# Attention and mixture of experts on one core: 804 slots for 816, and eight small moves in the schedule

## The chip, the core and the metric

The kernel runs on one core of one Trainium2 chip. The time is the device time of one launch in microseconds (us), and of several launches the median. A launch reads all inputs from the chip's main memory (HBM) and writes the output there. The profile is that of one further execution, recorded by the hardware profiler.

## The reference

Two layers follow one another. The first is attention over 4 batches, 8 heads, 768 positions and 64 elements a head: each query sees the keys within 15 positions of it, and beside them 24 summary keys, one for each block of 32 keys.

```
k_sum = k.reshape(B, H, nb, block, D).max(axis=3)
v_sum = v.reshape(B, H, nb, block, D).mean(axis=3)
scores_l = scale * q @ k^T          # kept where |i - j| < 16, else -1e9
scores_s = scale * q @ k_sum^T + log(32)
a = softmax(concat(scores_l, scores_s))
x = a @ concat(v, v_sum)
```

The result is read as 3072 tokens of 512 elements. The second layer sends each token to two of eight experts, chosen by noisy logits, and adds up what the two return.

```
noisy = x @ w_gate + log1p(exp(x @ w_noise)) * noise
two largest of each row -> experts, softmax over the two -> weights
out[token] += weight * (relu(x[token] @ w1[e]) @ w2[e])     # 512 -> 1024 -> 512
```

With 6144 places for eight experts an expert gets 768 tokens on average.

## The kernel before

**Attention** is worked through in 24 tiles of 128 queries, six to a batch. One turn of the loop, step t, holds work of several tiles: the division of tile t-1 (norm, L368), the scores and row maxima of tile t+2 (L322, L334), the transposes of the probabilities of tile t+1 (p_trans, L346), the exponentials of t+2 (sexp, L338), and the products with V of tile t in two halves (av, L357). Beside these stand side works. They are given to a list with a step number and a fraction, `at(t, f, ...)`, and the loop calls `run` with fixed fractions in a fixed order: 0.02, 0.03, 0.5, 0.1, 0.2, 0.09, 0.3, 0.32, 0.6, 0.85, 0, 0.8, 0.9. So a work at 10.85 stands near the end of step 10, ahead of one at 10.9, and one at 11 near the end of step 11. The works that the change touches:

- `load_k` (L107) brings the keys of a batch, two of its four head pairs at a time; `KL` says in which steps. The keys are kept in two buffers, one batch each. `k_piece` (L226) takes their block maxima on DVE; `KP` says when (the last batch in steps 11 to 14, third and fourth piece at 13.1 and 14.1).
- `kx_local` and `kx_sum` (L118, L126) copy the keys that one tile needs, and the block maxima, into one of `QN` buffers. The maxima are only copied for the first `QN` tiles of a batch, since they stay in the buffer.
- `v_sums` (L255) forms the block means of V on PE and copies them to the last 24 rows of a V buffer; `v_rest` (L287) copies them from there with DMAs to the other V windows (five for the third and the fourth batch). For the third batch the first stands at 10.6 and the second at 11.02. The products with V of a tile read both windows of its buffer.
- `w_load` (L664) brings a quarter of w1 or w2 of an expert (512 KB) into one of four stage buffers; `W0` says when the four w1 loads of expert 0 come. `w_part` (L686) then makes of each half a float16 high part on ACT and a float16 rest, the low half, on DVE.
- `norm_hi`, `norm_hi_dve`, `norm_lo` (L380 to L391) write a finished tile as a high and a low float16 part to one of three `xr` buffers, on ACT or DVE and on POOL; `x_out` (L393) stores it to HBM.
- `gate_f` and `gate_t` (L583, L590) build and multiply one-hot tables that tell for each slot of an expert which token it holds; `gate_t` is eight matmuls on PE, in the spare columns of the bank that holds a tile's result.

Each engine works its instructions off in the order of the program. All loads and stores of the attention stage are issued by SP's queue, in program order as well. At the start 90 products of the identity with itself (`warm_up`, L245) keep PE at work until the keys are there.

**Experts.** Each expert has `CAP` slots. The tokens of its slots are gathered with indirect DMAs in chunks of 128 (`x_gather`, seven chunks, `NCH`), and transposed with a DMA (`x_trans`, L813), the last chunk only as far as `CAP` reaches. The first layer of experts 1 to 7 (`mm1_all`, L887) is a seven-product scheme for a 2 x 2 split of its matrices (Strassen's): the slots are split in halves of `HC = CAP // 2`, and `product` (L858) runs each product as six matmuls of 128 x 128 by 128 x HC: high by high, low by high and high by low, two row groups each. Expert 0 uses the plain form (`mm1_pe`, L830), with the first `H0` = 384 slots ahead of the rest. The second layer takes chunks of 128 slots and 512 output columns (`mm2_pass`, L985); its last chunk has 64 slots, split into two column halves. What does not fit into `CAP` slots would be worked off in a branch at the end (L1452), which is entered only if an expert has more tokens than slots.

Of the kernel before, what the change touches and what calls it, by code (L numbers as in the profile page):

```python
# [9 lines left out]
F16 = mybir.dt.float16  # L10
# [10 lines left out]
P = 128  # L21
# [3 lines left out]
DM = H * D  # L25
E, F = 8, 1024
FC = F // P
DC = DM // P
# [3 lines left out]
PAD = WIN - 1  # L32
KW = 2 * (PAD + 1) + HP * S
VP = S + W - 64
H0, CAP = 384, 816
HF, HC = F // 2, CAP // 2
QN = 3
QBUF = 5
QA = 4
WARM = 90  # L40
SK = HP * NK
SW = 16 * (D + 1)
NCH = 7
# [17 lines left out]
def attn_moe(ctx, tc, qt, kt, vt, wgn, noise, w1, w2, out):  # L61
    nc = tc.nc
# [13 lines left out]
    moe = ctx.enter_context(tc.tile_pool(name="moe", bufs=1))  # L76
# [3 lines left out]
    work = works.enter_context(tc.tile_pool(name="work", bufs=2, side="right"))  # L80
# [19 lines left out]
    for i in range(2):  # L100
        KB.append(keep.tile([P, KW], F32, name=f"kb{i}"))
    for i in range(QN):
        KX.append(keep.tile([P, HP, 2, NK], F32, name=f"kx{i}"))
# [14 lines left out]
    def kx_local(t):  # L118
        b, j = divmod(t, TS)
        for blk in range(2):  # L120
            c = j * P + 64 * blk
            r = max(0, c + W - S)
            k = KB[b % 2][:, r:r + HP * S].rearrange("p (h s) -> p h s", h=HP)
            nc.gpsimd.tensor_copy(KX[t % QN][:, :, blk, 0:W], k[:, :, c - r:c - r + W])

    def kx_sum(t):  # L126
        b, j = divmod(t, TS)
        if j < QN:
            (nc.gpsimd if b else nc.vector).tensor_copy(KX[t % QN][:, :, :, W:NK],
                                                        KM[b][:, :, None, :].to_broadcast([P, HP, 2, NB]))  # L130
# [24 lines left out]
    identb = const.tile([P, P], BF, name="identb")  # L155
# [57 lines left out]
    late = []  # L213
# [29 lines left out]
    VO = []  # L243

    def warm_up(n):  # L245
# [2 lines left out]
            nc.tensor.matmul(o[:, i % 2, 0:P], identb, identb, start=True, stop=True, skip_group_check=True)  # L248
        VO.append(o)

    C4 = 2 * (D + 1)

    PV = {}
# [5 lines left out]
    def v_sums_pe(b):  # L259
# [5 lines left out]
        for j in range(TS):  # L265
            for g in range(4):
                nc.tensor.matmul(pt[32 * g:32 * g + NB, 0:C4], ind[:, j, :], VN[j][:, C4 * g:C4 * g + C4],  # L267
                                 start=(j == 0), stop=(j == TS - 1), skip_group_check=True)
# [35 lines left out]
    SC, PE_, PT, PO, X, XR, XT = {}, {}, {}, {}, {}, {}, {}  # L304
# [18 lines left out]
    def scores(t):  # L323
        s, q, k = SC[t], QR[t], KX[t % QN]
        for hp in range(HP):
# [54 lines left out]
    def norm_hi(t):  # L380
        if t in XR:
            return
        XR[t] = work.tile([P, 2 * DM], F16, name="xr", bufs=3)
        nc.scalar.activation(XR[t][:, 0:DM], X[t], AF.Copy)  # L384

    def norm_hi_dve(t):
        XR[t] = work.tile([P, 2 * DM], F16, name="xr", bufs=3)
        nc.vector.tensor_copy(XR[t][:, 0:DM], X[t])

    def norm_lo(t, engine=nc.gpsimd):  # L390
# [199 lines left out]
    def gate_t(b, o, i=1):  # L590
        tb = o[:, i, GO:GO + 3 * NS]
        n = (BATCH[b][1] - BATCH[b][0]) // GN
        for h in range(n):
            lh, rh, _ = GR[b, h]
            for j in range(GN):
                for k in range(2):
                    nc.tensor.matmul(tb, lh[:, 2 * j + k], rh[:, 2 * j + k],
                                     start=(h + k + j == 0), stop=(h == n - 1 and k == 1 and j == GN - 1),
                                     skip_group_check=True)
# [47 lines left out]
    def w_alloc(e):  # L647
        w1_alloc(e)
        w2_alloc(e)
# [127 lines left out]
    XTE = {}  # L777
# [34 lines left out]

    def x_trans(e, c):  # L813
        if c == 0:
            XTE[e] = (late[0] if e % 2 else moe).tile([P, 2 * DC, CAP], F16, name="xte")
        n = min(P, CAP - c * P)
        nc.sync.dma_start_transpose(out=XTE[e][:, :, c * P:c * P + n], in_=XC[e, c][:n])

    XC = {}
# [228 lines left out]
    def at(t, f, *a):  # L1048
        todo.setdefault(round(t, 3), []).append((f, a))
# [8 lines left out]

    warm_up(WARM)
    for t in range(1, 3):  # L1060
# [10 lines left out]
    at(0.1, v_sums_out, 0)  # L1071

    w_alloc(0)
    W0 = [6, 7, 11, 12]
    SPLIT = [7, 9, 13, 15]
    for i in range(4):
        at(W0[i], w_load, 0, i)
        for k in range(2):
            at(SPLIT[i] + k + 0.9, w_part, i, k, 0)
            at(SPLIT[i] + k + 2.1, w_part, i, k, 1)  # L1080
    VS = [4, 10, 16]
    KP = ((1, 1, 2, 2), (5, 6, 8, 8), (11, 12, 13, 14))
    KL = ((-1, 0), (3, 6), (9, 11))
    VL = [(1, 2), (7, 8), (13, 14)]
    for b in range(B - 1):
        for h in range(HP):
# [12 lines left out]
    for b, (t0, t1) in enumerate(BATCH[:4]):  # L1099
        u = t1 + 2  # L1100
        at(u - 0.15, gate_gt, b)
        at(u + 0.02, gate_gc, b)
        at(u + 0.09, gate_gl, b)
        at(u + 0.09, gate_gd, b)
        at(u + 0.9, gate_a, b)
        at(u + 1.1, gate_b, b)
        at(u + 1.1, gate_m, b)
        at(u + 1.9, gate_p, b)
        at(u + 2.3, lambda b, t: gate_c(b, PO[t]), b, u + 2)
        at(u + 3.02, lambda b, t: gate_d(b, PO[t]), b, u + 2)  # L1110
        at(u + 3.1, gate_e, b)
        if b == 3:
            break
        z = u + (6 if b < 2 else 4)
        at(z + 0.1 if b else u + 4.1, gate_v, b)
        at(z + (0.2 if b < 2 else 1.02), gate_o, b)
        at(z + 1.03, gate_f, b)
        at(z + 1.32, lambda b, t: gate_t(b, PO[t]), b, z + 1)
        at(z + 2.02, lambda b, t: gate_u(b, PO[t]), b, z + 1)
    at(20.1, decode, TB0, 0, 3)  # L1120
    at(20.85, gate_gt, 4)
# [17 lines left out]
    for t in range(-2, NT - 1):  # L1139
        if 3 <= t + QA < NT:  # L1140
            load_q(t + QA)
        if 1 <= t < NT - 2:
            v_load(t + 2)
        u = t + 3
        if t >= 1:
            norm(t - 1, (lambda: kx_sum(u)) if u < NT else None)
        run(t + 0.02)
        run(t + 0.03)
        if t + 2 < NT:
            scores(t + 2)  # L1150
        if 1 < u < NT and t < 1:
            q_piece(u)
        run(t + 0.5)
        if t + 2 < NT:
            smax(t + 2)
        if t in DVE_HI:
            norm_hi_dve(t - 1)
        if 0 <= t + 1 < NT:
            p_trans(t + 1, 0)
            p_trans(t + 1, 1)  # L1160
        if t + 3 < NT:
            mask_sums(t + 3)
        if t + 2 < NT:
            sexp(t + 2, 0)
        if u < NT and t >= 1:
            kx_local(u)
        run(t + 0.1)
        run(t + 0.2)
        if t >= 0:
            av_space(t)  # L1170
            av(t, range(H // 2))
        if t >= 1:
            x_pe(t - 1)
        run(t + 0.09)
        run(t + 0.3)
        run(t + 0.32)
        if t >= 1:
            x_copy(t - 1)
        if t + 2 < NT:
            sexp(t + 2, 1)  # L1180
        if t >= 1:
            norm_hi(t - 1)
            norm_lo(t - 1)
        if t >= 0:
            av(t, range(H // 2, H))
        run(t + 0.6)
        run(t + 0.85)
        run(t)
        run(t + 0.8)
        run(t + 0.9)  # L1190
        if t >= 2:
            x_out(t - 2)
# [142 lines left out]
    for e in range(1, E):  # L1335
# [8 lines left out]
        n = e + 1  # L1344
# [53 lines left out]
    def over_chunk(e, c):  # L1398
        tb = moe.tile([P, 2], I32, name="tbo", bufs=1)
        nc.sync.dma_start(tb, table[bass.ds(c * P + (e * R + CAP), P)])  # L1400
        idx = bass.IndirectOffsetOnAxis(ap=tb[:, 0:1], axis=0)
        x = XG[0]
        indirect(out=x, out_offset=None, in_=xd, in_offset=idx, bounds_check=N - 1, oob_is_err=False)
        pv = PREV[0]
        indirect(out=pv, out_offset=None, in_=out, in_offset=idx, bounds_check=N - 1, oob_is_err=False)
        xt = moe.tile([P, 2 * DC, CAP], F16, name="xte")[:, :, :P]
        nc.sync.dma_start_transpose(out=xt, in_=x)
        hh, hl = [x[:, :, :P] for x in HT]
        w = WT[e]
        for f in range(FC):  # L1410
            ph = bank()[:, 0, :P]
            k = 0
            for wn, xo in (("w1h", 0), ("w1l", 0), ("w1h", DC)):
                for d in range(DC):
                    nc.tensor.matmul(ph, w[wn][:, d, f * P:(f + 1) * P], xt[:, xo + d, :],
                                     start=(k == 0), stop=(k == 11))
                    k += 1
            nc.scalar.activation(hh[:, f, :], ph, AF.Relu)
            nc.vector.scalar_tensor_tensor(hl[:, f, :], ph, 0.0, hh[:, f, :], op0=OP.max, op1=OP.subtract)
        py = psum.tile([P, 512], F32, name="pt", bufs=2)  # L1420
        k = 0
        for wn, hx in (("w2h", hh), ("w2l", hh), ("w2h", hl)):
            for f in range(FC):
                wv = w[wn].rearrange("p a (b d) -> p (a b) d", d=DM)
                nc.tensor.matmul(py, hx[:, f, :], wv[:, f, :], start=(k == 0), stop=(k == 23))
                k += 1
        y = side_pool[0].tile([P, DM], F32, name="y", bufs=3)
        nc.vector.scalar_tensor_tensor(y, py, tb.bitcast(F32)[:, 1:2], pv, op0=OP.mult, op1=OP.add)
        indirect(out=out, out_offset=idx, in_=y, in_offset=None, bounds_check=N - 1, oob_is_err=False)
# [73 lines left out]
```

## Time and profile before

| | us |
|---|---|
| median of 3 runs (lowest, highest) | 659.13 (658.93, 660.64) |
| the profiled execution | 661.28 |
| its span, first to last instruction | 659.5 |
| PE busy in the span | 640.2 |
| DVE, ACT, POOL busy | 486.3, 319.3, 331.2 |
| attention: until the first product of expert 0 | 142.0 |
| expert 0: until the first product of expert 1 | 212.7 |

A row of the timeline has the start and the length in us, the engine, the line, the operation, the tiles (written <- read), the shape and the number of instructions in a run; in square brackets is the time that the engine stood idle before it and what ended that. A row of the chain of waits in order of time has start, length, engine, tile and line. A row of busy time by stretch has the stretch, its length, the busy time and number of instructions of PE, weight loads, DVE, ACT and POOL, then the granted clock of TensorE (1.00 is full), the busy share of the DMA engines and GB/s. A row of a group has the busy time of all its instructions and the mean of one in ns.

### The profile page before, as it was taken

The numbers are of one execution on the slowest core, as the hardware profiler recorded it, in microseconds if no ns is written. First come the engines' busy times: TensorE is split into PE (matmuls) and PEld (weight loads), VectorE is DVE, ScalarE is ACT, GpSimd is POOL, SyncE is SP. The second block draws the span as 40 slices with busy tenths as digits, with TensorE's granted clock in tenths as the row PEclk, the third lists the DMA queues.
The fourth block names the chain that finished last, engine by engine and source line by source line (L and its number), as shares of the span: only waits on it lengthen the run. The fifth ranks groups of instructions, "written<-read, shape, count | busy, mean of one in ns | idle before, by whom it ended". The sixth has DMA issues, their size and how long they took to land.

```text
span 659.5 us, 14051 instructions
## 1 busy us (share of the span) xinstructions
PE 640.2 (97%) x5407; PEld 372.2 (56%) x5407; DVE 486.3 (74%) x867; ACT 319.3 (48%) x677; POOL 331.2 (50%) x473
## 2 busy tenths in 40 slices
PE   7999899989999999999999999999999999999996
PEld 6777677755555554555455445544654555455543
DVE  5768889977788689587958795788678777856511
ACT  3889898753342653255326523542454155415400
POOL 5365444541856548563856376546556551632042
PEclk9999999999999999999999999999999999999999
DMA  8999997999998765536645664557257713431031
GB/s 301 307 298 319 286 326 254 288 257 363 243 191 166 228 190 160 205 116 194 168 162 177 160 198 151 182 157 229 96 190 164 239 70 113 144 126 49 1 106 44
DMA packets 104675, 125.58 MB, mean 190 GB/s; under 512 B 58525, under 2 KB 59813, under 8 KB 104600
## 3 DMA queue, kind: packets, MB, share of 16 engines
q1 hardware_dynamic: 92456, 88.32, 45.7%
q0 software_dynamic: 12144, 36.28, 17.3%
q8 instruction: 44, 0.72, 0.5%
q14 instruction: 31, 0.25, 0.1%
HBM read 87.57 MB, written 26.21 MB: 173 GB/s over the span
## 4 chain that ended last, share of the span: by engine, by line
PE 87%; ACT 4%; DMA 4%; DVE 3%; issue 1%; SPq 1%; POOL 1%; POOLq 0%; DVEq 0%
PE pt L994 37%; PE h L875 26%; PE h L839 5%; PE a L875 4%; PE pt L991 3%; PE s L329 2%; DMA kb<-in_kt_dram 2%; PE o L362 2%; PE pt L349 2%; ACT p L343 2%; PE pt L399 1%; DMA xg<-xd,tb 1%; PE h L994 1%; ACT pts L352 1%; PE pt L267 1%
## 5 line engine op out<-in xcount | busy, mean ns | idle before, releaser
L92 POOL DMA_INDIRECT out_dram<-y,tb x48 | 66.3, 1381 | 152.5 <-DVE y L1017 141.3
L994 PEld LDWEIGHTS <-hth 128*128 128x128 f16 x768 | 74.9, 98 | 89.2
L994 PE MATMUL pt<-w2h,hth 128*128 128x512 f16 x376 | 88.8, 379 | 0.0
L994 PE MATMUL pt<-w2h,htl 128*128 128x512 f16 x376 | 88.8, 379 | 0.0
L994 PE MATMUL pt<-w2l,hth 128*128 128x512 f16 x376 | 88.8, 379 | 0.0
L92 POOL DMA_INDIRECT xg<-xd,tb x53 | 70.4, 1328 | 31.3 <-DVE oc L614 17.4
L875 PE MATMUL h<-tx,sh 128*128 128x408 f16 x336 | 78.6, 336 | 0.0
L1017 DVE SCALAR_TENSOR_TENSOR y<-pt,tb,prev 128x512 f32<-128x512 f32 x42 | 31.5, 749 | 51.9 <-PE pt L994 51.9
L697 DVE SCALAR_TENSOR_TENSOR w2l<-stg,w2h 128x1024 f16<-128x1024 f32 x32 | 49.6, 1558 | 27.3 <-ACT w2h L680 27.3
L994 PEld LDWEIGHTS <-htl 128*128 128x128 f16 x384 | 37.6, 98 | 45.3
L875 PEld LDWEIGHTS <-w1h 128*128 128x128 f16 x448 | 43.3, 98 | 33.8 <-issue 1.4
L744 POOL TENSOR_TENSOR t<-xte 128x816 f32<-128x816 f16 x24 | 41.1, 1739 | 36.9 <-DVE t L700 31.6
L391 POOL TENSOR_TENSOR xr<-x,xr 128x512 f16<-128x512 f32 x24 | 28.9, 1205 | 59.4 <-ACT xr L384 36.7
L92 POOL DMA_INDIRECT prev<-out_dram,tb x42 | 51.9, 1236 | 13.6 <-issue 13.6
L875 PE MATMUL h<-xte,w1h 128*128 128x408 f16 x224 | 57.0, 336 | 0.0
L343 ACT ACTIVATE p<-s,nm 128x120 f32<-128x120 f32 x192 | 53.7, 378 | 0.8
L897 ACT ACTIVATE p<-h 128x408 f32<-128x408 f32 x28 | 14.3, 511 | 73.7 <-PE h L875 72.4
L772 ACT ACTIVATE tx<-t 128x816 f16<-128x816 f32 x28 | 24.0, 879 | 50.8 <-DVE t L700 50.8
L875 PEld LDWEIGHTS <-sh 128*128 128x128 f16 x336 | 32.9, 98 | 25.1
L875 PE MATMUL h<-tx,sl 128*128 128x408 f16 x168 | 42.7, 336 | 0.0
L883 DVE SCALAR_TENSOR_TENSOR htl<-h,hth 128x408 f16<-128x408 f32 x56 | 32.2, 575 | 8.3 <-ACT hth L880 8.2
L725 ACT ACTIVATE sh<-ws 128x1536 f16<-128x1536 f32 x14 | 20.8, 1483 | 35.7 <-DVE ws L700 27.7
(220 smaller groups left out, 1240.0 us busy)
## 6 DMA issues: line engine op xcount, KB each, us to landing
stg<-in_w_dram SPq DMA_DIRECT2D x62, 512.0 KB
q<-in_qt_dram SPq DMA_DIRECT2D x24, 256.0 KB
hth<-in_vt_dram SPq DMA_DIRECT2D x8, 768.0 KB
xd<-xr SPq DMA_DIRECT2D x24, 256.0 KB
out_dram<-prev SPq DMA_DIRECT2D x8, 768.0 KB
kb<-in_kt_dram SPq DMA_DIRECT2D x6, 768.0 KB
vw<-in_vt_dram SPq DMA_DIRECT2D x16, 260.0 KB
vw<-in_vt_dram SPq DMA_DIRECT2D x16, 130.0 KB
```

Source lines behind the costliest of these rows:

```text
L92: return nc.gpsimd.indirect_dma_start(**kw)
L343: nc.scalar.activation(PE_[t][:, a, hp, :], SC[t][:, a, hp, :], AF.Exp, bias=NM[t][:, 1, a, hp:hp + 1], scale=0.125)
L391: engine.tensor_tensor(XR[t][:, DM:], X[t], XR[t][:, 0:DM], op=OP.subtract)
L697: nc.vector.scalar_tensor_tensor(lo, SG[e, i], sc, hi, op0=OP.mult, op1=OP.subtract)
L725: nc.scalar.activation(h, x, AF.Copy, scale=W1S)
L744: nc.gpsimd.tensor_tensor(tt(e, 0 if low else j), xb(e, *i, low), xb(e, *o, low), op=OP.subtract)
L772: nc.scalar.activation(TX[e][:, 0, j - 1], t_of(e, j), AF.Copy)
L839: nc.tensor.matmul(ph[:, :n], w[wn][:, c, f * P:(f + 1) * P], x[:, xo + c, c0:c1], start=(k == 0), stop=(k == 11), skip_group_check=hook i ...
L875: nc.tensor.matmul(o, lhs[a][:, c], rhs[b][:, c], start=start and n == 0, stop=stop and n == 5, skip_group_check=True)
L883: nc.vector.scalar_tensor_tensor(HT[1][:, f, c0:c1], c, 0.0, HT[0][:, f, c0:c1], op0=OP.max, op1=OP.subtract)
L994: nc.tensor.matmul(py, hx[:, f, c * P:c * P + P], w[:, f, :], start=first, stop=final, skip_group_check=True)
L1017: nc.vector.scalar_tensor_tensor(y, py[:, :d], gw, pv[:, :d], op0=OP.mult, op1=OP.add)
```

## The change

`CAP` goes from 816 to 804, and with it `HC` from 408 to 402. The transposed tokens keep their width of 816 (`XCAP`), and the DMA transpose of the last chunk still takes 48 rows, of which 36 are gathered; the rest of the row is not read. `QN` goes from 3 to 2, the `xr` buffers from 3 to 4. There are 100 warming products for 90, and ten more after the scores of tile 1 and ahead of the transposes of tile 0. The third w1 load of expert 0 stands at 10.9 for 11, the second half of the last batch's keys at 10.85 for 11. The low halves of w1 stood at 9.1, 10.1, 11.1, 12.1, 15.1, 16.1, 17.1, 18.1 and now stand at 10.1, 10.2, 13.1, 13.2, 15.1, 16.1, 18.1, 19.1. The table product of the third group of tiles stands at 19.6 for 19.32, behind the second half of the products with V.

```diff
-H0, CAP = 384, 816
+H0, CAP = 384, 804
+XCAP = 816
 HF, HC = F // 2, CAP // 2
-QN = 3
+QN = 2
 QBUF = 5
 QA = 4
-WARM = 90
+WARM = 100
...
+    def keep_warm(n):
+        for i in range(n):
+            nc.tensor.matmul(VO[0][:, 1, 0:P], identb, identb, start=True, stop=True, skip_group_check=True)
+
...
     def norm_hi(t):
         if t in XR:
             return
-        XR[t] = work.tile([P, 2 * DM], F16, name="xr", bufs=3)
+        XR[t] = work.tile([P, 2 * DM], F16, name="xr", bufs=4)
...
     def x_trans(e, c):
         if c == 0:
-            XTE[e] = (late[0] if e % 2 else moe).tile([P, 2 * DC, CAP], F16, name="xte")
-        n = min(P, CAP - c * P)
+            XTE[e] = (late[0] if e % 2 else moe).tile([P, 2 * DC, XCAP], F16, name="xte")
+        n = min(P, XCAP - c * P)
...
-    W0 = [6, 7, 11, 12]
+    W0 = [6, 7, 10.9, 12]
     SPLIT = [7, 9, 13, 15]
+    LOW = ((10.1, 10.2), (13.1, 13.2), (15.1, 16.1), (18.1, 19.1))
     for i in range(4):
         at(W0[i], w_load, 0, i)
         for k in range(2):
             at(SPLIT[i] + k + 0.9, w_part, i, k, 0)
-            at(SPLIT[i] + k + 2.1, w_part, i, k, 1)
+            at(LOW[i][k], w_part, i, k, 1)
     VS = [4, 10, 16]
     KP = ((1, 1, 2, 2), (5, 6, 8, 8), (11, 12, 13, 14))
-    KL = ((-1, 0), (3, 6), (9, 11))
+    KL = ((-1, 0), (3, 6), (9, 10.85))
...
-        at(z + 1.32, lambda b, t: gate_t(b, PO[t]), b, z + 1)
+        at(z + (1.32 if b < 2 else 1.6), lambda b, t: gate_t(b, PO[t]), b, z + 1)
...
         if t in DVE_HI:
             norm_hi_dve(t - 1)
+        if t == -1:
+            keep_warm(10)
         if 0 <= t + 1 < NT:
             p_trans(t + 1, 0)
             p_trans(t + 1, 1)
```

More of the change, by code (lines that the diff above doesn't have):

```diff
@@ L382, in norm_hi @@
             return
-        XR[t] = work.tile([P, 2 * DM], F16, name="xr", bufs=3)
+        XR[t] = work.tile([P, 2 * DM], F16, name="xr", bufs=4)
         nc.scalar.activation(XR[t][:, 0:DM], X[t], AF.Copy)
     def norm_hi_dve(t):
-        XR[t] = work.tile([P, 2 * DM], F16, name="xr", bufs=3)
+        XR[t] = work.tile([P, 2 * DM], F16, name="xr", bufs=4)
         nc.vector.tensor_copy(XR[t][:, 0:DM], X[t])
@@ L1405, in over_chunk @@
         indirect(out=pv, out_offset=None, in_=out, in_offset=idx, bounds_check=N - 1, oob_is_err=False)
-        xt = moe.tile([P, 2 * DC, CAP], F16, name="xte")[:, :, :P]
+        xt = moe.tile([P, 2 * DC, XCAP], F16, name="xte")[:, :, :P]
         nc.sync.dma_start_transpose(out=xt, in_=x)
```

## The prediction

> **What bounds the kernel now.** I read the page's summary and its chain of waits first, then that chain in order of time, and last the timeline and the busy time by stretch of the stages that the edits touch.
>
> ```profile
> span 659.5 us, 14051 instructions
> PE 640.2 (97%) x5407; PEld 372.2 (56%) x5407; DVE 486.3 (74%) x867; ACT 319.3 (48%) x677; POOL 331.2 (50%) x473
> PE 87%; ACT 4%; DMA 4%; DVE 3%; issue 1%; SPq 1%; POOL 1%; POOLq 0%; DVEq 0%
> ```
>
> TensorE sets the end for 87% of the span. How evenly it does so in the experts is seen in the chain in order of time (start, length, what, how many), and in the busy time of the stretch from 212 us on.
>
> ```profile
> 176.85 17.52 PE h L839 x96
> ...
> 227.25 12.42 PE h L875 x72
> 241.74 31.08 PE pt L994 x144
> 212.00:660.00 448.00, 441.06 (x2532) 231.23 (x2528) 316.71 (x430) 182.07 (x296) 223.99 (x293) 1.00 0.50 150
> L875 PE MATMUL h<-tx,sh 128*128 128x408 f16 x336 | 78.6, 336 | 0.0
> ```
>
> From 212 us PE is busy 441 of 448 us, DVE 317, ACT 182, POOL 224, and the products stand end to end: 12.42/72 = 172.5 ns for 408 columns, 17.52/96 = 182.5 ns for 432. So a column costs (182.5 - 172.5)/24 = 0.417 ns. (The 336 ns of one product is its latency; products overlap, and no idle time stands before them.) A column taken out here is time taken off the end. In the attention stage, up to 142 us, the chain changes between PE, ACT, DVE and transfers, so there an edit is worth what its own step says.
>
> **804 slots.** The seven-product scheme of experts 1 to 7 runs 7 experts x 4 row blocks x 7 products x 6 matmuls = 1176 matmuls, each half of the slots wide: 402 columns for 408. That is 6 x 0.417 = 2.5 ns each, 2.94 us in all. Expert 0's second half falls from 432 to 420 columns in 96 matmuls: 96 x 12 x 0.417 = 0.48 us. Sum **-3.42 us**. The second layer does not change: its last chunk is computed 64 slots wide in both kernels. What DVE, ACT and POOL save on 402 columns lies beside PE. The other end of the bound is that the narrower slices stream no faster (0); I take the full 3.42, since the two rows that bracket it, 408 and 432, lie on PE without idle time. In the reference's own draw of inputs the fullest expert gets 801 tokens and expert 0 ends at slot 748, so 804 suffices and the overflow branch, 48 table writes at some 1.4 us each and eight weight reloads, stays shut.
>
> The rows above were taken with slices that begin at multiples of 816 bytes; 804 leaves 4 bytes over a multiple of 16. The Trainium skill, "SBUF — State Buffer", section "Specifications (TRN2)", says that SBUF is read in lines of 16 bytes and that each crossing into a new line pays a penalty; by that rule a shifted slice touches one line more, no run here shows such a slice, and the sum would lose part of the 3.42 us. It is the third rival below.
>
> **Warming products.** Ten more stand at the start and ten between the scores and the first transposes of tile 0.
>
> ```profile
> 1.55 6.92 PE L248 MATMUL o<-identb 128*128 128x128 bf16 x90 [1.55 <-DVE identb L156]
> ...
> 10.73 0.44 PE L329 MATMUL s<-kx,q 64*64 64x120 f32 x8 [1.10 <-DVE kx L241]
> 11.20 1.05 PE L329 MATMUL s<-kx,q 64*64 64x120 f32 x32
> 13.10 2.09 PE L349 MATMUL pt<-ident,p 128*120 128x128 f32 x8 [0.84 <-ACT p L343]
> 15.30 1.68 PE L329 MATMUL s<-kx,q 64*64 64x120 f32 x32
> 16.91 2.64 PE L267 MATMUL o<-hth 128*24 128x130 f32 x48
> 22.39 1.05 PE L329 MATMUL s<-kx,q 64*64 64x120 f32 x32
> 70.53 1.53 PE L267 MATMUL pt<-hth 128*24 128x130 f32 x48 [0.79 <-ACT xt L405]
> 8.60:12.00 3.40, 2.30 (x72) 1.82 (x68) 3.10 (x7) 0.00 (x0) 2.83 (x8) 1.00 1.06 410
> 12.00:15.40 3.40, 2.56 (x27) 1.37 (x23) 1.64 (x3) 2.92 (x11) 0.36 (x1) 1.00 1.08 332
> 15.40:18.90 3.50, 3.50 (x74) 2.87 (x70) 1.16 (x1) 2.64 (x10) 0.00 (x0) 0.51 0.98 232
> ```
>
> Ten products at 6.92/90 = 77 ns are 0.8 us. The first ten lie under the 1.10 us that the scores wait for the keys at 10.73, the other ten in the 0.84 us before 13.10, where PE waits for ACT: cost **0**, and 1.6 us if both covers went. What they could gain: from 15.4 to 18.9 the granted clock is 0.51. The scores there take 1.68 us instead of 1.05, the V sums 2.64 instead of 1.53: 1.7 us at most. The stretch before it (12.0 to 15.4) had PE busy 2.56 of 3.40 us and lost the clock all the same; the one before, with 2.30, kept it. So busy time as such doesn't decide, and whether 0.8 us more would is not shown. I take **0** (the row as it stands) and keep -1.7 for the range.
>
> The Trainium skill, "TensorE: Matmul & The Clock Gate", Part 4, says that transposes do not count as busy for the clock, which fits the eight transposes that fill most of the stretch lost. Part 1 adds that the windows run free of the kernel's start, which speaks against a steady gain: the same ten products would fall on another side of a window from run to run. By the rule that activity holds the clock the sum would be 1.7 us lower, by the free-running window it would be so in some executions only.
>
> **The two loads one step sooner.** The second half of the last batch's keys and the third w1 load go from after step 11's copies of the V sums (L292) to before step 10's x_out, on SP's queue.
>
> ```profile
> 69.12 0.61 SPq L301 DMA_DIRECT2D vw<-in_vt_dram  x1
> 70.41 0.33 SPq L394 DMA_DIRECT2D xd<-xr  x1
> ...
> 74.52 2.63 SPq L292 DMA_DIRECT2D vw<-vw  x3
> ...
> 78.71 0.52 SPq L671 DMA_DIRECT2D stg<-in_w_dram  x1
> 79.28 1.59 SPq L110 DMA_DIRECT2D kb<-in_kt_dram  x1
> 79.30 0.69 DVE L377 TENSOR_TENSOR x<-o,ri 128x512 f32<-128x512 f32 x1
> 80.09 0.69 PE L362 MATMUL o<-vw,pts 120*64 120x65 f32 x16 [0.94 <-issue]
> ...
> 86.82 0.95 DVE L232 TENSOR_REDUCE kmax<-kb 128x24 f32<-128x768 f32 x1 [0.96 <-DMA kb<-in_kt_dram]
> 88.59 1.05 PE L329 MATMUL s<-kx,q 64*64 64x120 f32 x32 [0.58 <-DMA q<-in_qt_dram]
> 85.00:85.50 0.50, 0.50 (x11) 0.43 (x8) 0.50 (x1) 0.44 (x1) 0.50 (x1) 1.00 1.06 410
> stg<-in_w_dram SPq DMA_DIRECT2D x62, 512.0 KB
> kb<-in_kt_dram SPq DMA_DIRECT2D x6, 768.0 KB
> ```
>
> The keys were issued at 79.28 and released DVE at 86.82, 7.5 us later: a transfer waits behind those ahead of it. What it removes: DVE's 0.96 us at 86.82 and most of PE's 0.58 us at 88.59. What it adds: x_out, the next queries, V of tile 13 and the five copies of L292 now stand behind 1280 KB, which at 410 GB/s (85.0 to 85.5) take 1.31/0.41 = 3.2 us. Of these only the first copy is urgent: it fills the second window of tile 12's V, and the attention products of tile 12 read it at 80.09. The copy was issued at 74.52, so it had 5.6 us, no more than its neighbours needed; it landed just in time, and its place in the order is what is late next. Behind that product on PE wait the transposes, the next scores and so the row maxima on DVE, the engine that is nearly full here. Bounds: 0 if the copy had been there 3.2 us before 80.09, 3.2 if it landed at 80.09. Two things work on it afterwards: the waits of 0.96 and 0.58 that are gone, and the moved low halves of w1 (next part). I take **+2.0**: 3.2 less 1.5, and 0.3 for the low halves.
>
> **Low halves, buffers, table product.**
>
> ```profile
> 68.93 0.56 DVE L388 CAST xr<-x 128x512 f16<-128x512 f32 x1 [1.53 <-DMA xd<-xr]
> L690 DVE SCALAR_TENSOR_TENSOR w1l<-stg,w1h 128x512 f16<-128x512 f32 x8 | 6.3, 791 | 0.0
> L129 POOL COPY kx<-kmax 128x192 f32<-128x192 f32 x9 | 4.8, 539 | 0.0
> 120.03 0.74 PE L597 MATMUL o<-rh,lh 128*128 128x168 f16 x8 [0.65 <-DVE rh L585]
> 142.55 0.63 ACT L384 ACTIVATE xr<-x 128x512 f16<-128x512 f32 x1 [1.63 <-DMA xd<-xr]
> ```
>
> The low halves are the same eight instructions of 0.79 us. One leaves each of the steps 9, 11, 12 and 17; two more stand in step 13 and one more each in 10 and 19. Those out of 11 and 12 leave DVE before the late copy, where it then waits anyway; the two in step 13 (1.58 us) come after it. That is the 0.3 above, with 0 and 1.6 as its ends. A fourth xr buffer removes DVE's 1.53 us at 68.93 and ACT's 1.63 us at 142.55. The first lies ahead of the late copy, which swallows it; behind the second stand matmuls of expert 0 that PE runs meanwhile: **-0.2**, ends 0 and -1.5. Two kx buffers for three save three of POOL's copies (3 x 0.54 us) and one of DVE's; the buffer that is rewritten is that of the tile whose scores ran a step earlier, so nothing new waits: **0**. The eight table products of batch 2 move behind the second half of the attention products, and PE's 0.65 us at 120.03 is covered by them: **-0.65**, other end 0, since DVE is what PE waits for.
>
> **Sum:** -3.42 + 0 + 2.0 - 0.2 - 0.65 = -2.3 us, made against the span of 659.5 us (the profiled execution took 661.28 with what lies around it). On the median of 659.13 this gives **656.8 us**.
>
> **Rivals.**
> 1. *The late copy costs nothing.* It lands early enough, or the stages up to 128 us have room for it. For: the 0.94 us before 80.09 ends 0.1 us after DVE's 79.30 + 0.69, so DVE may have been the cause. Then the two waits come back as gains: -3.42 - 0.2 - 0.65 - 0.96 = -5.2, 653.9 us.
> 2. *The clock holds at the start.* For: the 0.84 us gap is filled. Against: the queries and V arrive at a pace set by transfers, which the edit leaves. Half of 1.7 arrives: 656.0 us.
> 3. *Slices of 402 read slower* (slower than before). Place: the 1176 products of L875. If their new starts (every 804 bytes for 816) made each as long as the 432-column row, 182.5 for 170.0 ns, it would cost 14.7 us: 671.5. It decides from 2.0 ns per product on, where the 2.3 us are gone. Against: a product streams columns, and nothing in the rows shows memory as its pace.
> 4. *The stall in full.* 3.2 us with both low halves behind it, 4.8 in all, and the queries no earlier: 659.13 - 3.42 - 0.85 + 4.8 = 659.7 us; or, at the same place, 804 slots that save nothing: 660.2.
>
> **How the numbers follow.** The forecast has 0.35 (its own range 655.5 to 658.5), rival 1 0.32, rival 2 0.14, rival 3 0.04, rival 4 0.15. The range of 653.4 to 659.8 reaches to rivals 1 and 4 and leaves out rival 3 and the tails. A change under 0.3%, 2.0 us, is about what a measurement can't tell from none. Below 657.15 lie 0.19 of the forecast, 0.31 of rival 1 and 0.11 of rival 2: 0.61. Between lie the forecast's other 0.16, 0.01 and 0.03 of these two and 0.12 of rival 4: 0.32. Above 661.1 lie rival 3 and 0.03 of rival 4: 0.07.
>
> **What would show it.** Right: L875 at 170 ns a product; tile 12's attention products waiting some 2 to 3 us; no wait for kb or q in step 13; no wait for xd at L388 and L384; L597 without its 0.65. Wrong: the time from the span's start to expert 0's first product shorter than 141 us, which is rival 1 or 2; a clock of 1.00 from 15.4 on; L875 above 172 ns.

## The result, and the profile after

The changed kernel takes 663.32 us (median of 9 runs, 662.59 to 665.11), the kernel before beside it 659.61 us (9 runs, 657.69 to 662.31): a ratio of **1.0059, 95% interval 1.0045 to 1.0072**. It is 3.7 us slower, where 2.3 us faster was forecast. The profiled execution took 662.59 us with a span of 660.7 us. That is the fastest of its nine, while the profile of before (661.28 us) lies above the median of its kernel, so the two profiles show less of a difference than the medians do: 1.2 us of span for 3.7 us.

Two rows of the page of the changed kernel, its span and the busy times:

```profile
span 660.7 us, 14089 instructions
...
PE 640.1 (97%) x5427; PEld 373.6 (57%) x5427; DVE 480.9 (73%) x866; ACT 317.7 (48%) x677; POOL 330.8 (50%) x470
```

PE has 20 products more and is busy as long as before (640.1 for 640.2 us), although 1272 of its products are shorter: part of them must have become slower somewhere. The timeline of the changed kernel shows where, by the first product of expert 0 and the chain of waits by the first of expert 1 and the long runs of products (start, length, what, how many):

```profile
145.91 0.83 PE L844 MATMUL h<-xte,w1h 128*128 128x384 f16 x4
```

```profile
180.78 17.04 PE h L844 x96
216.10 1.13 PE h L880 x6
...
230.53 12.30 PE h L880 x72
...
606.19 12.30 PE h L880 x72
```

Expert 0 starts at 145.91 us for 142.0 before: **3.9 us are lost in the attention stage**, and 2.7 us come back from there to the span's end (660.7 - 145.9 = 514.8 us for 659.5 - 142.0 = 517.5). Such a difference between two single profiles is not sure by itself: three kernels of the experiments whose attention stage is scheduled as before (804, 806 and 808 slots) start expert 0 at 140.48, 139.94 and 143.86 us. So it has to be found where in the stage the time goes.

The loss stands in step 12. Timeline of the changed kernel, SP's queue and then PE and DVE (in brackets the idle time before, and what ended it):

```profile
70.52 0.73 SPq L111 DMA_DIRECT2D kb<-in_kt_dram  x1
71.29 0.50 SPq L676 DMA_DIRECT2D stg<-in_w_dram  x1
71.89 1.36 SPq L399 DMA_DIRECT2D xd<-xr  x1
...
75.89 3.14 SPq L297 DMA_DIRECT2D vw<-vw  x3
...
79.33 0.69 DVE L382 TENSOR_TENSOR x<-o,ri 128x512 f32<-128x512 f32 x1
80.12 0.30 PE L367 MATMUL o<-vw,pts 120*64 120x65 f32 x2 [0.15 <-issue]
82.86 0.88 PE L367 MATMUL o<-vw,pts 120*64 120x65 f32 x14 [2.44 <-DMA vw<-vw]
86.02 0.17 DVE L376 TENSOR_SCALAR r<-o 128x8 f32<-128x8 f32 x1 [3.77 <-PE o L367]
86.53 0.69 DVE L382 TENSOR_TENSOR x<-o,ri 128x512 f32<-128x512 f32 x1
...
89.90 0.67 DVE L695 SCALAR_TENSOR_TENSOR w1l<-stg,w1h 128x512 f16<-128x512 f32 x1
...
92.56 0.68 DVE L695 SCALAR_TENSOR_TENSOR w1l<-stg,w1h 128x512 f16<-128x512 f32 x1
...
93.66 0.69 DVE L382 TENSOR_TENSOR x<-o,ri 128x512 f32<-128x512 f32 x1
```

The keys and the w1 quarter now go out ahead of x_out. The copies of V's means follow at 75.89 for 74.52, and tile 12's products with V, ready at 80.12 as before, do two of sixteen and wait 2.44 us for the first copy. Then comes what the forecast did not have. Busy time by stretch (PE, weight loads, DVE, ACT, POOL, then granted clock, DMA share, GB/s):

```profile
79.80:83.20 3.40, 0.81 (x16) 0.53 (x14) 2.44 (x4) 2.42 (x9) 2.05 (x3) 1.00 0.69 204
83.20:86.60 3.40, 3.40 (x52) 3.08 (x51) 0.44 (x3) 1.77 (x6) 0.00 (x0) 0.50 0.84 220
```

PE was busy 0.81 of 3.40 us, and the next 3.40 us run at **half clock**, PE being busy all of it while DVE has 0.44 us of work. So the wait is paid twice. The kernel before divided its tiles 12 and 13 at these times:

```profile
83.23 0.69 DVE L377 TENSOR_TENSOR x<-o,ri 128x512 f32<-128x512 f32 x1
...
89.39 0.69 DVE L377 TENSOR_TENSOR x<-o,ri 128x512 f32<-128x512 f32 x1
```

Tile 11 stands at 79.33 for 79.30, tile 12 at 86.53 for 83.23 (+3.3), tile 13 at 93.66 for 89.39 (+4.3), behind the two low halves of w1 that the change moved to this place. Of the 4.3 us, 3.9 are left at expert 0's first product.

### The profile page after: what moved, and what is told of

Read it like the earlier page. It is cut to its first block, busy times and chain, and to the rows that moved or that the text cites. A ratio compares the mean times of both kernels' runs of the same rounds, so it can differ in the third digit from the quotient of the medians.

```text
span 660.7 us, 14089 instructions
## 1 busy us (share of the span) xinstructions
PE 640.1 (97%) x5427; PEld 373.6 (57%) x5427; DVE 480.9 (73%) x866; ACT 317.7 (48%) x677; POOL 330.8 (50%) x470
## 4 chain that ended last, share of the span: by engine, by line
PE 87%; ACT 4%; DVE 4%; POOL 2%; issue 2%; DMA 1%; POOLq 0%; DVEq 0%
PE pt L999 37%; PE h L880 26%; PE h L844 5%; PE a L880 4%; PE pt L996 3%; PE o L367 2%; PE pt L354 2%; PE s L334 2%; ACT p L348 2%; PE o L249 1%; PE pt L404 1%; DMA vw<-vw 1%; DVE nm L341 1%; PE h L999 1%; PE pt L422 1%
## 5 line engine op out<-in xcount | busy, mean ns | idle before, releaser
L880 PE MATMUL h<-tx,sh 128*128 128x402 f16 x336 | 78.0, 333 | 0.0
L702 DVE SCALAR_TENSOR_TENSOR w2l<-stg,w2h 128x1024 f16<-128x1024 f32 x32 | 47.7, 1498 | 28.9 <-ACT w2h L685 28.9
L749 POOL TENSOR_TENSOR t<-xte 128x804 f32<-128x804 f16 x24 | 39.2, 1658 | 37.4 <-DVE t L705 33.4
L880 PE MATMUL h<-xte,w1h 128*128 128x402 f16 x224 | 56.4, 333 | 0.0
L902 ACT ACTIVATE p<-h 128x402 f32<-128x402 f32 x28 | 14.2, 506 | 74.0 <-PE h L880 72.4
L777 ACT ACTIVATE tx<-t 128x804 f16<-128x804 f32 x28 | 23.7, 869 | 50.4 <-DVE t L705 50.4
L880 PE MATMUL h<-tx,sl 128*128 128x402 f16 x168 | 42.2, 332 | 0.0
L888 DVE SCALAR_TENSOR_TENSOR htl<-h,hth 128x402 f16<-128x402 f32 x56 | 31.8, 569 | 8.3 <-ACT hth L885 8.3
```

The lines of the kernel that those rows point to most:

```text
L702: nc.vector.scalar_tensor_tensor(lo, SG[e, i], sc, hi, op0=OP.mult, op1=OP.subtract)
L749: nc.gpsimd.tensor_tensor(tt(e, 0 if low else j), xb(e, *i, low), xb(e, *o, low), op=OP.subtract)
L777: nc.scalar.activation(TX[e][:, 0, j - 1], t_of(e, j), AF.Copy)
L880: nc.tensor.matmul(o, lhs[a][:, c], rhs[b][:, c], start=start and n == 0, stop=stop and n == 5, skip_group_check=True)
L888: nc.vector.scalar_tensor_tensor(HT[1][:, f, c0:c1], c, 0.0, HT[0][:, f, c0:c1], op0=OP.max, op1=OP.subtract)
```

## Experiments

Each kernel is compared with the kernel before on the same chip. Ratios are of the medians, with 95% intervals. The rows come from several chips: rows two to five from one, PE kept busy and the copy on POOL with the low halves back from a second, the other four from a third; for the first row no chip is on record. A quotient of two rows from different chips is less sure than the rows: one such quotient below shows 0.26% where one chip shows nothing.

| kernel | ratio | 95% interval |
|---|---|---|
| the change | 1.0059 | 1.0045 to 1.0072 |
| the change, both loads back | 0.9978 | 0.9952 to 1.0004 |
| before, with both loads sooner | 1.0106 | 1.0067 to 1.0144 |
| before, with 804 slots | 0.9971 | 0.9952 to 0.9991 |
| the change, one copy on POOL | 0.9979 | 0.9963 to 0.9995 |
| the change, PE kept busy in step 12 | 1.0009 | 0.9983 to 1.0034 |
| the change, only the keys sooner | 1.0010 | 0.9989 to 1.0030 |
| copy on POOL, low halves back | 0.9953 | 0.9926 to 0.9979 |
| the same, rows of tx 816 bytes | 0.9951 | 0.9935 to 0.9968 |
| the same, low halves moved again | 0.9951 | 0.9933 to 0.9970 |
| rows of tx 816, low halves back, 3 kx and 3 xr buffers | 0.9948 | 0.9929 to 0.9966 |

**Both loads back.**

```diff
-    W0 = [6, 7, 10.9, 12]
+    W0 = [6, 7, 11, 12]
-    KL = ((-1, 0), (3, 6), (9, 10.85))
+    KL = ((-1, 0), (3, 6), (9, 11))
```

> The changed kernel with the two loads back at the end of step 11. Theory A (the late copy of V's means, with the cold clock behind it, is the whole loss of the attention stage): tile 12's products with V no longer wait 2.44 us, the clock is 1.00 from 25 us on, expert 0 starts some 4 us sooner, at 142 us, and the time is that of 804 slots alone, about 657 us (-2.4 on the kernel before). Rival B (other edits cost too: two kx buffers, or the new idle 1.29 us of PE at 62 us): expert 0 starts at 143 us or later, and the time is 658 us or more. Rival C (the loads are not to blame): it stays at 662 to 663 us.

Measured: 0.9978, 1.4 us below the kernel before. In the timeline tile 12's products run in one piece, and expert 0 starts at 141.62 us:

```profile
79.22 0.69 PE L367 MATMUL o<-vw,pts 120*64 120x65 f32 x16 [0.49 <-issue]
...
141.62 0.82 PE L844 MATMUL h<-xte,w1h 128*128 128x384 f16 x4
```

The loads turn a gain of 0.2% into a loss of 0.6%: 1.0059/0.9978 = 1.0081, 5.3 us (3.4 to 7.3, from the two intervals). Rival C falls. Of A and B, the time leaves both open (its interval takes in the 657 of the one and the 658 of the other). Expert 0 starts where A said, at 142, and not at 143 or later, which speaks for A but, by the spread of single profiles above, does not settle it. The same step can be compared tile by tile, by the divisions of the tiles 11, 12 and 13:

```profile
78.43 0.69 DVE L382 TENSOR_TENSOR x<-o,ri 128x512 f32<-128x512 f32 x1
...
81.77 0.69 DVE L382 TENSOR_TENSOR x<-o,ri 128x512 f32<-128x512 f32 x1
...
88.47 0.69 DVE L382 TENSOR_TENSOR x<-o,ri 128x512 f32<-128x512 f32 x1
```

Tile 12 comes 3.3 us after tile 11, where the change takes 7.2, and tile 13 10.0 us after it, for 14.3.

**The loads alone**, the two lines above the other way round in the kernel before.

> The kernel before with the two loads one step sooner and nothing else. Theory A: the wait of tile 12's products for the copy appears (2 to 2.5 us) and the clock drops behind it for 3.4 us; expert 0 starts at about 145 us, and the time is some 3 us above the kernel before, 662.5 us. Rival B (the loads alone cost little, as the stage has room for a late copy): under 660.5 us, expert 0 before 143 us.

Measured: 1.0106, 7.0 us, twice what was expected; expert 0 starts at 145.52 us, as expected. PE's timeline and the busy time by stretch:

```profile
81.82 1.13 PE L362 MATMUL o<-vw,pts 120*64 120x65 f32 x14 [2.67 <-DMA vw<-vw]
```

```profile
76.94:80.34 3.40, 1.12 (x9) 0.52 (x8) 3.19 (x11) 2.20 (x7) 2.05 (x3) 1.00 0.93 317
80.34:83.75 3.41, 1.93 (x18) 1.79 (x19) 1.23 (x3) 0.86 (x4) 0.00 (x0) 0.50 0.78 221
83.75:87.16 3.41, 3.41 (x56) 2.93 (x54) 1.80 (x5) 2.12 (x6) 0.93 (x1) 0.50 0.79 250
```

The same wait, in a kernel without any of the other edits, and here two stretches at half clock, since the wait reaches into the second.

**804 slots alone** (`CAP` and `XCAP` as in the change).

> The kernel before with 804 slots and nothing else. Theory A: the attention stage is unchanged (expert 0 starts at 142.0 us); a product of the seven-product scheme takes 170.8 ns and not the 170.0 that a price per column gives, so the time falls by some 2.4 us (-0.37%) to 657.1 us. Rival (each column counts): 170.0 ns, -3.4 us, 656.1 us. Rival (804 saves nothing): 172.5 ns and 659.5 us.

Measured: 0.9971, -1.9 us (-3.2 to -0.6). The products of the seven-product scheme take 12.30/72 = 170.8 ns, as in the changed kernel, so theory A has the price of a product and the two rivals fall. Its other part did not come true: expert 0 starts at 140.48 us and not at 142.0, in an attention stage without an edit. This kernel's profiled execution has a stall of its own, which is told in the last section.

**One copy on POOL.** The loads stay sooner; the copy that fills the second window of tile 12's V needs no transfer any more.

```diff
-        for y in x[2 if b == 1 else 1:]:
+        for y in x[2 if b < 3 else 1:]:
             nc.sync.dma_start(y, x[0])
+    def v_second(b):
+        x = v_slots(b)
+        nc.gpsimd.tensor_copy(x[1], x[0])
...
+        if b == 1:
+            at(VS[b] + 1.1, v_second, b + 1)
```

> The changed kernel, loads still sooner, but the first of the five copies of V's means of the third batch (the one that fills the second window of tile 12's V) is made by POOL and not by a transfer. Theory A (that one copy is what is late): tile 12's wait is gone or under 0.6 us, the clock stays at 1.00 there, and the time is that with the loads back, 657 to 658 us. Rival (the stage as a whole is behind because transfers are late): another transfer is waited for in steps 12 to 13, such as the queries or V of tile 13, and less than 2 of the 4 us come back.

Measured: 0.9979, the same as with the loads back. From its timeline:

```profile
73.15 0.62 POOL L301 COPY vw<-vw 24x520 f32<-24x520 f32 x1
...
78.61 0.69 PE L371 MATMUL o<-vw,pts 120*64 120x65 f32 x16
...
80.84 1.05 PE L338 MATMUL s<-kx,q 64*64 64x120 f32 x32 [0.23 <-DMA q<-in_qt_dram]
```

All sixteen products run without a wait, and the one that follows next, for the queries, is 0.23 us. One copy of 24 rows was late; the stage as a whole was not.

**PE kept busy.** The copy stays late, but 40 products of the identity stand ahead of tile 12's products with V.

```diff
             av_space(t)
+            if t == 12:
+                for i in range(40):
+                    nc.tensor.matmul(PO[t][:, 1, 0:P], identb, identb, start=True, stop=True, skip_group_check=True)
             av(t, range(H // 2))
```

> The changed kernel with 40 more products of the identity on PE at the head of tile 12's products with V, so that PE is busy while the late copy is under way; nothing else is moved, and the copy stays late. Theory A (the stall is paid twice: first the wait, then 3.4 us or more at half clock, because PE stood idle): the clock stays at 1.00 in step 12, PE is held up by the copy as before, and 1 to 2 us of the loss come back: about 0.2 to 0.3% under the changed kernel, some 0.3% above the kernel before. Rival (the clock costs nothing, since DVE and ACT set the pace there): the time stays 0.6% above the kernel before.

Measured: 1.0009. Timeline and stretches:

```profile
82.85 0.68 PE L367 MATMUL o<-vw,pts 120*64 120x65 f32 x14 [1.27 <-DMA vw<-vw]
...
144.33 0.82 PE L844 MATMUL h<-xte,w1h 128*128 128x384 f16 x4
```

```profile
78.70:82.10 3.40, 2.77 (x46) 2.43 (x42) 2.38 (x4) 2.35 (x8) 2.05 (x3) 1.00 0.67 191
82.10:85.50 3.40, 2.65 (x67) 2.48 (x71) 0.47 (x3) 1.34 (x5) 0.00 (x0) 1.00 0.77 227
```

The copy lands when it did (82.85 for 82.86), the clock stays at 1.00, and 14 products take 0.68 us for 0.88. Work that computes nothing takes 0.50% off the change (0.9950, 0.9921 to 0.9979: 1.4 to 5.2 us, where 1 to 2 were expected; a quotient of two chips). The two profiles give 1.6 us: from the copy's landing to expert 0's first product it is 61.5 us (144.33 - 82.85) for 63.1 (145.91 - 82.86). So the clock is a part of the loss beside the wait, and the rival falls; whether it is the smaller or the larger part is not settled.

That the clock is lost not only in the profiled execution is seen from the mean granted clock, which is on record for each execution of the change and of the experiments. The profiles tell how to read it: the mean is 0.997 to 0.999 in those without a stretch of 3.4 us at half clock ahead of the last microseconds, 0.994 to 0.996 in those with one, and 0.992 in those with two. The nine executions of the change have 0.987 to 0.996, the middle one 0.992; the kernel before, in 79 executions beside the experiments, 0.993 to 0.999, middle 0.998. With the loads back the middle is 0.997, with the loads alone 0.992, with the copy on POOL 0.9965, with PE kept busy 0.9975. So a usual execution of the change or of the loads alone loses the clock about twice, and a usual one of the kernel before, with the loads back or with PE kept busy, not at all.

**Only the keys sooner** (`W0` back at 11, `KL` as changed).

> The changed kernel with the third w1 load back at the end of step 11 and only the keys one step sooner: 768 KB ahead of the copy of V's means for 1280 KB. Theory A (the copy is late by what stands ahead of it in the queue): 512 KB at 0.41 MB/us are 1.25 us, so the wait of tile 12 falls from 2.44 us to about 1.2 us, too short for the clock to drop, and the time lies between the kernel with both loads back (-0.2%) and the changed kernel (+0.6%): about 0.1% above the kernel before. Rival (the stall is not a matter of size): 2 us or more remain, and the time stays at +0.5% or more.

Measured: 1.0010, where it was expected, but not by the way expected:

```profile
73.97 2.63 SPq L297 DMA_DIRECT2D vw<-vw  x3
...
80.62 0.68 PE L367 MATMUL o<-vw,pts 120*64 120x65 f32 x14 [1.78 <-DMA vw<-vw]
```

```profile
78.00:81.40 3.40, 1.47 (x23) 1.01 (x22) 2.66 (x4) 2.63 (x9) 2.05 (x3) 1.00 0.58 138
81.40:84.80 3.40, 3.40 (x53) 3.20 (x56) 1.20 (x5) 2.12 (x6) 0.33 (x1) 0.50 1.02 335
```

With 512 KB less in front, the wait is 0.66 us shorter and not 1.25, and the clock drops here too. A price per byte can't be taken from that: the copies were also issued 1.92 us sooner, and from the issue to the product that waited it is 6.65 us here, 6.97 in the change and 7.99 with PE kept busy, behind the same 1280 KB as in the change. What the times follow is the clock. Five of the twelve executions had a mean clock of 0.997 or more and took 658.2 to 659.7 us; the other seven had 0.995 or less and took 660.0 to 664.3 us. Of the nine of the change none was above 0.996. So the shorter wait loses the clock in about half of the executions, the longer one in nearly all; how the 0.49% between the two kernels (1.0059 for 1.0010) is shared by wait and clock is not shown.

**How the narrower slices are read**: 806 and 808 slots in the kernel before, and then, in the changed kernel with the copy on POOL and the low halves of w1 at their old places, rows of 816 bytes in the tile `tx`.

```diff
-        TX[e] = side_pool[0].tile([P, 2, 4, 2, HC], F16, name="tx")
+        TX[e] = side_pool[0].tile([P, 2, 4, 2, XCAP // 2], F16, name="tx")[:, :, :, :, :HC]
```

> The kernel before with 806 slots, slices of 403 columns. If columns are charged in fours (402 as 404): 170.8 ns a product, the same as with 804 slots. If each column counts and the new starts cost 0.8 ns besides: 171.2 ns. If columns are charged in twos: 171.6 ns.

> The kernel before with 808 slots, slices of 404 columns. If columns are charged in fours: 170.8 ns a product, the same as with 804 and 806 slots. If each column counts and the new starts cost 0.8 ns besides: 171.6 ns.

> The changed kernel with POOL's copy of V's means for tile 12, the low halves of w1 at their old places, and the tile tx (the sums of token blocks that the seven-product scheme reads) with rows of 816 bytes, of which 804 are used, so that each slice of it starts at a multiple of 16 bytes. Theory S (a slice that starts off a multiple of 16 bytes costs 1 to 2 ns a product): products on tx fall from 171 to 172 ns to 170.0, the stretch of 72 products from 12.30 us to about 12.24, and the whole by 0.8 us; time 0.4 to 0.6% below the kernel before. Rival (402 columns cost 170.8 ns wherever they start): 12.30 us as before.

The kernels with 806 and 808 slots ran once each (659.67 and 667.82 us), which says nothing of their time. Rows of the chain of waits, 806 and 808 slots, and 804 with rows of 816 bytes:

```profile
226.38 12.39 PE h L876 x72
...
603.16 12.38 PE h L876 x72
```

```profile
234.91 12.35 PE h L876 x72
...
611.30 12.35 PE h L876 x72
```

```profile
225.36 12.24 PE h L884 x72
...
600.28 12.24 PE h L884 x72
```

That is 172.1 ns for 403 columns, 171.5 for 404, and 170.0 for 402 with aligned rows (170.8 without). Charging in fours falls: 402, 403 and 404 differ. Over the price per column (0.417 ns) they pay 0.8, 1.7 and 0.7 ns. With rows of 816 bytes the same 402 columns take what the forecast said, 170.0 ns, so the surcharge hangs on the rows of `tx`. That a start off a multiple of 16 bytes is its cause is not shown. By the starts of the products in the trace of the change, those that read `tx` (672 of the 1176) take 171.2 ns on average and those that read `xte` 170.0. Among the latter, the slices of the second half of the slots also start off 16 bytes, 804 bytes into a row of 1632, and take 169.7. Over a whole expert, from the first of these rows to the seventh: before (quoted start 227.25; the row of its seventh stands below) 62.9 us, changed 62.6 us, padded 62.5 us.

```profile
604.75 12.42 PE h L875 x72
```

(604.75 - 227.25)/6 = 62.92; (606.19 - 230.53)/6 = 62.61; (600.28 - 225.36)/6 = 62.49. Times seven experts, the change saves 2.1 us and the padded kernel 3.0, the 2.94 us of the forecast. In time the padded kernel stands at 0.9951; 0.8 us cannot be told from the 0.9953 of the same kernel unpadded, which was measured on another chip.

**The low halves of w1.** First at their old places in the changed kernel with the copy on POOL, then, with rows of 816 bytes, moved again.

```diff
-    LOW = ((10.1, 10.2), (13.1, 13.2), (15.1, 16.1), (18.1, 19.1))
+    LOW = ((9.1, 10.1), (11.1, 12.1), (15.1, 16.1), (17.1, 18.1))
```

> The changed kernel with POOL's copy of V's means for tile 12, and the low halves of w1 at their old places (steps 9 to 12 and 15 to 18). Theory A (the two low halves in step 13 cost up to 1.6 us, as DVE is nearly full there): tile 13's division is no later against tile 12's than before, and the time is 0.5 to 1.5 us below the same kernel with the low halves moved, 0.3 to 0.4% below the kernel before. Rival (their place costs nothing): within 0.5 us of it, -0.2%.

> The same with the low halves of w1 where the change puts them (two in step 13). Theory (they cost up to 1.6 us in step 13): the time lies 0.5 to 1.5 us above the kernel with the low halves at their old places, and tile 13's division is later by that much. Rival (their place costs nothing): within 0.5 us.

Measured: 0.9953 for 0.9979 on different chips, which looked like a gain; on one chip 0.9951 for 0.9951 (656.52 and 656.76 us). In the two profiles of this chip the low halves do delay tile 13, as the theory said: its division comes 6.7 us after tile 12's for 5.1. But tile 12's comes 0.6 us sooner after tile 11's, and at expert 0's first product 0.6 us is left (141.43 for 140.79). In the time their place costs nothing that can be measured, with intervals of some 1.1 us either way.

**Three kx and three xr buffers** (a third kx and a fourth xr buffer do not fit together), with rows of 816 bytes and the low halves at their old places.

> POOL's copy, old places of the low halves, rows of 816 bytes in tx, and besides three kx and three xr buffers as in the kernel before (a fourth xr buffer and a third kx buffer do not fit together). Theory (buffers cost and gain nothing): within 1 us of the same kernel with two kx and four xr buffers, and the waits of DVE at tile 11 and of ACT at the end of the attention for the store of xr come back. Rival (the fourth xr buffer was worth its 1.5 us): that much slower. Rival (two kx buffers cost at the start): that much faster.

Measured: 656.19 us, 0.9948, for 656.52 us with two and four: no difference. The waits for the store of xr are back (0.81 us on DVE, 0.46 on ACT) and do not show in the time. This kernel and the two before it lie 0.5% below the kernel before (this one 0.9929 to 0.9966) and, by the ratios, 1.1% below the change: 804 slots with aligned rows and earlier loads, without a late copy.

## Why the prediction was wrong, point by point

**The step that failed** is the price of the two loads: "I take +2.0: 3.2 less 1.5, and 0.3 for the low halves". The wait was forecast rightly: the copy named, its place in the queue, the tile, and "tile 12's attention products waiting some 2 to 3 us" (2.44). The size of the whole was wrong: the trace has 4.3 us from tile 11 to tile 13, the times 5.3 us and 7.0 us. A cost that follows the wait had no term, and what was set against the wait did not come.

First, what an idle PE does to its clock. The forecast read the clock row at 15.4 us and asked only what the warming products could gain; it did not ask what a wait of 3 us would lose. Its upper bound of 3.2 us was the length of the wait, and the half clock afterwards lay outside it. The runs with PE kept busy and with the loads alone show this, and the mean clocks of all executions. The Trainium skill, "TensorE: Matmul & The Clock Gate", Part 1, says that the clock halves after one idle window of about 3.4 us and that the windows run free. The length agrees (3.40 us at 0.50 in the changed kernel). That the window must be idle does not: PE was busy 0.81, 1.12 and 1.47 of 3.40 us in the three stretches that lost it, and the measurement decides.

Second, the 1.5 us credited for the waits for kb and q, and the 0.3 us for the low halves. Both waits are gone, as forecast, but tile 13 is no better off against tile 12: it loses another 1.0 us (4.3 for 3.3). The waits were not a fixed cost of the kernel before. Of the four profiles with its attention stage two have the wait for kb (before and 806 slots, 6.2 and 6.4 us from tile 12's division to tile 13's); 804 and 808 slots do not, and take 5.1 and 5.2 us. And in the same place now stand the two moved low halves: all six kernels that move them take 6.6 to 7.1 us there, whether the loads come sooner or not (6.7 with the loads back). So the credit was 1.0 to 1.3 us in some executions, and the low halves took it back at this place. Earlier keys would have been worth little here in any case, as DVE had just waited 3.77 us for PE; that is argued, no run shows it.

**804 slots**: -3.42 forecast; 2.1 us on the seven experts and 0.48 us on expert 0 (17.52 - 17.04) make **-2.6**, and 2.7 us by the spans. The price per column was right. What was mis-sized is the length of the products that read `tx`, whose rows stand 804 bytes apart: 171.2 ns and not 170.0, which is 0.8 us in all. The forecast cited a rule beside it (the Trainium skill, "SBUF — State Buffer", section "Specifications (TRN2)": lines of 16 bytes, with a penalty for each crossing), put it among the rivals at 14.7 us and left it out of the sum. That "the sum would lose part of the 3.42 us" came true, but not for the reason given: 804 bytes touch 51 lines of 16 bytes whether they start 0, 4, 8 or 12 bytes into a line, so "a shifted slice touches one line more" is wrong, and the shifted slices of `xte` pay nothing (169.7 ns). Why the rows of `tx` cost something stays open. By direction rival 3 was true, with 0.8 us for its 14.7, too little to decide.

**Warming products**: 0 forecast, and nothing can be shown of them. The kernels without the new products (the loads alone, 804 alone) keep the clock at the start as well; of the kernel with 804 alone:

```profile
12.00:15.40 3.40, 3.16 (x48) 2.05 (x52) 0.78 (x1) 3.37 (x13) 0.00 (x0) 1.00 1.09 315
15.40:18.90 3.50, 3.32 (x72) 2.56 (x70) 2.76 (x6) 3.16 (x12) 0.58 (x1) 1.00 1.03 228
```

The half clock from 15.4 on belonged to the profiled execution of before, not to the kernel. In the changed kernel the clock drops one stage later, at 21.8. Rival 2 falls, and the reading that the clock moves from run to run stands.

**Buffers, low halves, table product**: 0, 0.3, -0.2 and -0.65 forecast. Low halves and buffers showed nothing in the time. The waits for xd at L388 and L384 are gone, and so is L597's 0.65 us, but the last tile's division shows no gain: it stands 4.5 us later than before (142.83 us for 138.36), tile 13's 4.3. The likely reading is that the -0.85 us were waits of engines that were not the bound; no run moves the table product alone. "Nothing new waits" for the second kx buffer was not quite so: in this one profile the scores of tile 3 wait for POOL's copy of the keys, which other kernels with two buffers do not show.

```profile
21.42 1.61 PE L334 MATMUL s<-kx,q 64*64 64x120 f32 x32 [1.53 <-POOL kx L125]
```

**Rivals and chances.** Rival 4, the stall in full, named the course; it had 0.15 and ended at 659.7 or 660.2 us, since it knew the wait and the low halves but not the clock. Rival 1 is refuted by 2.44 us. With the terms as measured the sum is -2.6 for the slots and +5.3 for the loads, +2.7 of the 3.7 us; the last 1 us is inside the intervals and is not assigned. Why the times put 5 to 7 us on the loads where the trace has 4.3 is open in part. The 4.3 us are counted from tile 11, and in the profile of the change tile 11 stands late, behind a stretch at half clock at the start: at 79.33 us, and at 78.17 with PE kept busy, where the clock held. The copy was waited for until the same time in both (82.86 and 82.85), so a late tile 11 hides a part of the wait. In which stages the other executions lost their clock is not shown.

## What to carry to other kernels

Before a load is moved up in a queue, find the smallest transfer behind it that an engine reads within the next stage, and price not only the wait but what follows: here TensorE, after it had been busy for 0.8 to 1.5 of 3.4 us, ran at half clock for 3.4 us or more, and a cheap way out is to take that one transfer off the queue (here a copy of 0.62 us on POOL). When a tile is cut, try the narrower slice in rows of the old length too: here rows of 816 bytes let 402 columns save what they cost, and rows of 804 did not. A wait seen in one profile counts as a gain only if other profiles of the kernel have it and nothing new stands in its place.

## What the runs showed of the hardware

- **Rows of 804 bytes.** Products with 402 columns on `tx` take 171.2 ns on average with rows of 804 bytes and 170.0 with rows of 816. The surcharge lies on the second of the two row groups: from the start of the first to that of the second it is 169.8 ns, from there to the next start 172.6. Slices of `xte` that start 804 bytes into a row pay nothing. In stretches of 72 products, 54 of them on `tx`, 402, 403 and 404 columns pay 0.8, 1.7 and 0.7 ns over the price per column.
- **How little idle time the clock needs.** Stretches of 3.4 us with PE busy 0.81, 1.12 and 1.47 us were followed by half clock; with 2.77 us it stayed. One dropped after a stretch in which PE was busy longer: 1.74 us, at the start of the changed kernel. Before, 2.30 us had held it there, and 2.56 us, most of them transposes, had not. In two other profiles 1.89 and 1.93 us held it (low halves moved again, 18.36 to 21.77 us; 806 slots, 173.63 to 177.04 us), so the busy time alone gives no threshold. The drop at the start of the changed kernel:

```profile
18.36:21.76 3.40, 1.74 (x45) 1.49 (x49) 1.38 (x4) 2.54 (x10) 3.34 (x6) 1.00 1.01 329
21.76:25.17 3.41, 3.41 (x40) 2.58 (x32) 2.00 (x3) 0.81 (x2) 0.11 (x1) 0.50 1.03 382
```

- **Waits without a releaser.** In the changed kernel PE stands still for 1.29 us inside tile 9's products, with nothing that the profile shows to wait for.

```profile
63.56 0.51 PE L367 MATMUL o<-vw,pts 120*64 120x65 f32 x10 [1.29 <-issue]
```

With PE kept busy the same product waits 1.33 us. With the loads back it does not, but there the transposes at 42.18 us wait 1.25 us, and seven other kernels wait 1.05 to 1.25 us ahead of the same transposes. So such waits have fixed places in the program and show at only some of them in one execution. Their cause is open.

- **A stall ahead of expert 0's second half.** In the profile of 804 slots alone, ACT's copy of the last transposed rows starts 2.6 us late with a releaser that the profile doesn't know, and PE waits 4.47 us for it and runs at half clock after it:

```profile
179.28 0.49 ACT L827 ACTIVATE xte<-h 128x384 f16<-128x384 f16 x1 [2.62 <-remote]
179.82 1.56 PE L840 MATMUL h<-xte,w1h 128*128 128x420 f16 x4 [4.47 <-ACT xte L827]
```

At the same place PE waits 1.48 us with 806 and 3.25 us with 808 slots. Before and after the change the wait is absent. Its cause is open. It is one reason why a single profile of such a kernel says little of a change of 0.3%.
